# A new instruction order for an attention and mixing kernel, from a planner with other prices for changes between matmul kinds, and a fifth warm-up matmul

## The chip, the cores and the metric

The kernel runs on one core of a Trainium2 chip. The metric is device time in microseconds (us), from the first instruction to the last, for one execution. Five engines work beside each other and wait for one another by semaphores: TensorE (PE in the profile, with PEld for its weight loads), VectorE (DVE), ScalarE (ACT), GpSimd (POOL) and SyncE (SP), which here only issues transfers.

## What is computed

Four sequences of 448 tokens, twelve heads of 64, model width 768. Causal attention gives `x`, and a mixing layer follows it:

```python
scores = scale * np.matmul(q, k.transpose(0, 1, 3, 2))      # q, k, v: (4, 12, 448, 64)
scores = np.where(mask, -1000000000.0, scores)              # causal
attn = np.exp(scores - np.max(scores, axis=-1, keepdims=True))
attn = attn / (np.sum(attn, axis=-1, keepdims=True) + 1e-09)
x = np.matmul(attn, v)                                       # laid out as (4, 448, 768)

theta = x @ w_theta
zr, zi = x * np.cos(theta), x * np.sin(theta)
y = np.einsum('ts,bsd->btd', w_tok_r, zr) + np.einsum('ts,bsd->btd', w_tok_i, zi)
u = x + y
out = u + np.maximum(u @ w_ch, 0.0)
```

## The kernel before

**Attention** goes by quads, four heads at a time, three quads to a sequence, twelve in all (`load_quad`, `attend`). `load_quad` issues the transfers of a quad on SP (line 498): two tiles of q (`qs`), two of k (`kk`), two of v (`vs`), each with a pair of heads; of the first quad the q tiles come in two parts, columns 0 to 255 and 256 to 447. `attend` then makes the scores in seven blocks of 64 query rows, in four groups (`SG`): every block is four matmuls on quarters of the array, 64 by 64, two heads by two key halves (line 638, into `s`, `t` or `m` tiles of PSUM; the program calls this kind "q"). DVE adds the mask and finds the row bound (line 647, with a second small instruction that reads the accumulator), ACT takes the exponential and the row sum (line 650). PE transposes the results (line 683, kind "t", four 128 by 128 transposes into one `t` tile, of which there are two), ACT (line 515) or DVE (line 517) copies each `t` tile into `pta` or `ptb`, and PE multiplies by v (line 713, kind "x", 64 columns of the array for each of `pta` and `ptb`, into the one `xo` tile). The row sums go another way: ACT adds a small number (line 658), DVE takes the reciprocal (line 659), PE transposes it (line 660), DVE copies it to `rs` (line 661), and two transfers, `rd` and `rb`, spread it over the partitions. DVE multiplies `xo` by `rb` into `xT` (line 716) and so frees `xo` for the next pair.

**Weights** come as 64-bit floats. `weight` brings one block (`raw`), and ACT (line 539) and DVE (lines 542 twice, 545) make 32-bit floats of it (`zw`); a rounded high part is cast (line 515 or 517) and the rest is subtracted (line 523, POOL or DVE). The six blocks of `w_theta` and the seven of `w_tok` are decoded while attention runs.

**The layer**: `theta` multiplies by `w_theta` (line 766, `th`, kind "m"), then follow the sine and cosine, transposes of x (lines 825 and 826, `xp`, kind "t"), products on DVE (828, 830), a split into high and low parts (`zh`, `zl`), the token mixing (line 845, `y`, kind "m"). `pair` makes the last product (lines 943 and 953, `cp`) for two sequences together with fewer block products, and writes the output.

**The order.** Nothing of this order is written out by hand. Each operation is given to `P.op` with its engine or a choice of engines, its duration, and a due time; `Plan.order` plays the operations through once, each engine taking the ready one with the earliest due time, and the resulting list is issued as it stands. `SHIFT` moves the due time of a group of operations, `PEN` says how willingly a group is given to its second engine. `TURN` is the price in ns that the planner adds when PE goes from one kind of matmul to another (rows and columns in the order m, t, x, q), and it prefers a ready operation whose change is cheaper among those nearly as early. `QO` is an extra per score block, `gp` the price of a two-operand instruction on POOL, `tab` the activation table that ACT holds at the start, and `NW` the number of warm-up matmuls (`warm`, line 1041: 16 by 256 on zeros), which PE runs before the first scores.

Of the kernel before, what the change touches and what calls it, by code (L numbers as in the profile page):

```python
# [24 lines left out]
          PR=2, AE=19487.722, BB=6550.4261, AP=172724.4184, AQ=41305.8643, XT=3, NQ=8, WP=2, NW=4, EX=-0.0, PORT=1,  # L25
# [9 lines left out]
QO = 15.0  # L35
TURN = ((0, 0, 145, 288), (0, 0, 145, 288), (106, 56, 0, 87), (108, 120, 54, 0))


SHIFT = {2: 99415, 3: 9107, 4: -2529, 5: -6011, 6: -4744, 7: -5690, 8: 36879, 9: -6000, 10: 1863, 11: 9305, 12: 767, 13:
# [157 lines left out]
class Plan:  # L197
# [67 lines left out]
    def order(self):  # L265
# [15 lines left out]

        free = {}
        port = wire = 0.0
        tab = [None]
        last = ["m"]

        def turn(a, b):
# [37 lines left out]
        while done < len(self.ops):  # L325
# [3 lines left out]
            while ev and ev[0][0] <= t:  # L329
                _, kind, _, x = heapq.heappop(ev)  # L330
# [63 lines left out]
def attention_moe_kernel(  # L394
# [22 lines left out]
    NQ = NP // 2  # L417
# [71 lines left out]
    def gp(n):  # L489
        return 2.2 * n + 300  # L490
# [664 lines left out]
```

## Time and profile before

| | us |
|---|---|
| median of three runs | 441.61 |
| the three runs | 441.84, 441.20, 441.61 |
| the profiled execution, its own time | 441.63 |
| its span in the profile | 439.8 |
| PE busy in the span | 425.3 (97%) |
| DVE busy | 358.7 (82%) |
| ACT busy | 241.8 (55%) |
| POOL busy | 55.1 (13%) |
| mean granted TensorE clock | 0.992 |

The span counts from the first to the last instruction of the profile; 1.8 us of the execution's own time lie around it. A matmul in 32-bit floats is shown as one or two records, and a record's duration reaches from its start to the end of its passage through the array, so that records overlap: what one instruction costs PE is read from the start of one to the start of the next. The share of busy time of an engine says nothing of single stages.

### The profile page before, as it was taken

What the parts mean: (1) busy time and instruction counts of PE and PEld (TensorE: products, weight loads), DVE (VectorE), ACT (ScalarE), POOL (GpSimd) and SP (SyncE); (2) the same over time, 40 slices, a digit from 0 to 9 for tenths busy, and PEclk for the clock granted to TensorE, in tenths of its full rate; (3) what the DMA queues carried; (4) which work ended last, traced back from release to release, by engine and by line L of the source; (5) the groups of instructions that cost most, each with busy time, mean ns of one, the idle gap of its engine ahead of it and who ended that gap; (6) DMA issues with size and microseconds to landing.
All of it is one profiled execution on the core that took longest, in us unless ns stands there. A gap on an engine that the chain in (4) does not pass through costs nothing.

```text
span 439.8 us, 8190 instructions
## 1 busy us (share of the span) xinstructions
PE 425.3 (97%) x2927; PEld 354.3 (81%) x2927; DVE 358.7 (82%) x928; ACT 241.8 (55%) x602; POOL 55.1 (13%) x48
## 2 busy tenths in 40 slices
PE   8679999999999999999999999999999999999996
PEld 4347766969996686788899878979999879999995
DVE  3889999688986668679993679869569998799886
ACT  3789999389836547486830589624054533233220
POOL 2131123000000000000000000006012323231420
PEclk9889999999999999999999999999999999999999
DMA  7866785313547235152323110331533312035214
GB/s 241 306 205 232 240 255 177 106 43 109 178 148 239 87 109 165 58 163 67 99 94 143 55 57 12 110 102 36 179 110 89 104 57 90 2 105 175 98 43 146
DMA packets 33953, 55.34 MB, mean 126 GB/s; under 512 B 10361, under 2 KB 27641, under 8 KB 33913
## 3 DMA queue, kind: packets, MB, share of 16 engines
q1 hardware_dynamic: 33912, 54.82, 38.9%
q8 instruction: 23, 0.38, 0.3%
q14 instruction: 18, 0.14, 0.1%
HBM read 41.55 MB, written 11.69 MB: 121 GB/s over the span
## 4 chain that ended last, share of the span: by engine, by line
PE 86%; DVE 9%; DMA 2%; issue 1%; ACT 1%; SPq 0%; DVEq 0%; ACTq 0%
PE y L845 22%; PE th L766 20%; PE cp L943 15%; PE xo L713 10%; PE t L683 8%; PE s L638 4%; PE t L638 4%; PE xp L825 2%; DVE e L647 2%; DMA raw<-w_theta 1%; DMA qs<-q 1%; DVE R L788 1%; DVE C L828 1%; DVE zw L542 1%; DVE zl L523 1%
## 5 line engine op out<-in xcount | busy, mean ns | idle before, releaser
L766 PE MATMUL th<-wth,xs 128*128 128x384 f32 x528 | 106.1, 344 | 0.0
L845 PE MATMUL y<-wtk,zh 128*128 128x448 f32 x336 | 98.1, 373 | 0.5 <-DVE R L830 0.5
L766 PEld LDWEIGHTS th<-wth,xs 128*128 128x128 f32 x528 | 90.1, 188 | 5.2 <-issue 3.3
L650 ACT ACTIVATE e<-e,sm 128x64 f32<-128x64 f32 (+6 forms) x168 | 83.3, 498 | 17.5 <-DVE sm L647 17.3
L845 PEld LDWEIGHTS y<-wtk,zh 128*128 128x128 f32 x336 | 60.9, 188 | 5.7 <-issue 0.8
L845 PE MATMUL y<-wtk,zl 128*128 128x448 f32 x168 | 61.5, 366 | 0.0
L683 PE MATMUL t<-ident,e 128*128 128x128 f32 x336 | 48.4, 280 | 5.2 <-ACT e L650 3.2
L713 PE MATMUL xo<-pta,vs 128*64 128x448 f32 (+1 forms) x192 | 48.8, 394 | 2.3 <-DVE xT L716 2.3
L713 PE MATMUL xo<-ptb,vs 128*64 128x448 f32 (+1 forms) x192 | 48.8, 394 | 0.0
L683 PEld LDWEIGHTS t<-ident,e 128*128 128x128 f32 x336 | 39.5, 143 | 10.8 <-issue 2.4
L713 PEld LDWEIGHTS xo<-pta,vs 128*64 128x64 f32 x192 | 24.4, 139 | 27.3 <-issue 14.9
L943 PE MATMUL cp<-ub,wth 128*128 128x448 f32 x207 | 45.1, 366 | 0.0
L943 PEld LDWEIGHTS cp<-ub,wth 128*128 128x128 f32 x207 | 38.8, 188 | 3.1
L647 DVE CUSTOM_DVE_ANT_0 e<-s,mask 128x64 f32<-128x64 f32 (+3 forms) x96 | 31.2, 366 | 10.2 <-PE s L638 10.0
L943 PE MATMUL cp<-ub,wa 128*128 128x448 f32 x162 | 37.0, 366 | 0.0
L523 POOL TENSOR_TENSOR ub<-xT,ub 128x448 fp32r<-128x448 f32 x5 | 12.0, 2402 | 180.2 <-DVE ub L517 170.6
L845 PEld LDWEIGHTS y<-wtk,zl 128*128 128x128 f32 x168 | 31.5, 188 | 2.9
L943 PEld LDWEIGHTS cp<-ub,wa 128*128 128x128 f32 x162 | 30.2, 188 | 2.2
L650 ACT ACTIVATION_READ_ACCUMULATOR e<-e,sm 128x1 f32 x168 | 31.5, 188 | 0.0
L647 DVE CUSTOM_DVE_ANT_0 e<-t,mask 128x448 f32<-128x448 f32 (+2 forms) x60 | 27.3, 498 | 0.8 <-PE t L638 0.5
L515 ACT CAST ub<-tt 128x448 fp32r<-128x448 f32 x19 | 10.6, 567 | 30.2 <-PE cp L943 17.0
L638 PE MATMUL s<-kk,qs 64*64 64x64 f32 (+3 forms) x384 | 24.7, 368 | 1.1 <-DMA qs<-q 1.0
(108 smaller groups left out, 670.9 us busy)
## 6 DMA issues: line engine op xcount, KB each, us to landing
vs<-v SPq DMA_DIRECT2D x24, 256.0 KB
kk<-k SPq DMA_DIRECT2D x24, 224.0 KB
rb<-rd SPq DMA_DIRECT2D x48, 112.0 KB
qs<-q SPq DMA_DIRECT2D x22, 224.0 KB
raw<-w_theta SPq DMA_DIRECT2D x6, 768.0 KB
raw<-w_ch SPq DMA_DIRECT2D x6, 768.0 KB
wd<-zc SPq DMA_DIRECT2D x6, 768.0 KB
wf<-wd SPq DMA_DIRECT2D x24, 192.0 KB
```

Of the source, the lines that this page charges most:

```text
L515: alts.append((e, ac(n, 0 if psum else 1), lambda: nc.scalar.copy(out=o(), in_=i())))
L523: P.op([(e, gp(n) if e == "POOL" else dv(n), lambda e=e: ENG[e].tensor_tensor(out=o(), in0=a(), in1=b(), op=op)) for e in engs], r=r, w=w, ...
L542: P.op("DVE", dv2(n) + 20, lambda i=i, c=c, op=op: nc.vector.tensor_scalar(out=half(z.t[:, 1], 2)[:, :, i], in0=half(raw.t, 4)[:, :, 2 * i ...
L638: nc.tensor.matmul(out=ss[a].t[D * i:D * i + D, c:c + w], lhsT=qp[i].t[own, D * x:D * x + D], rhs=kp[i].t[own, S - w:S] if a else kp[i].t[ ...
L647: P.op("DVE", dv(w) + 8, lambda a=a, c=c, w=w, y=y, e=e, s=ss[a]: nc.vector.tensor_tensor_reduce(out=e.t[:, w * a:w * a + w], in0=s.t[:, c ...
L650: P.op("ACT", ac(w, 2.5), lambda a=a, w=w, y=y, e=e: nc.scalar.activation(out=e.t[:, w * a:w * a + w], in_=e.t[:, w * a:w * a + w], func=A ...
L683: nc.tensor.transpose(ps.t[:, 128 * y:128 * y + 128], E[x].t[:, c:c + 128], ident)
L713: nc.tensor.matmul(out=xo.t[D * a:D * a + D, 128 * j:S], lhsT=vs[i].t[:, c:c + D], rhs=pt[a].t[:, i, D * SLOT[j]:D * SLOT[j] + w], start=( ...
L766: nc.tensor.matmul(out=th.t[:, 0:HW], lhsT=l, rhs=wth[:, p, w2, c0:c0 + HW], start=(p == 0 and n == 0), stop=(p == KD - 1 and n == len(ops ...
L825: nc.tensor.transpose(xp.t[:, t], x.t[:, g, 128 * t:128 * t + 128], ident)
L845: nc.tensor.matmul(out=y.t[:, 0:S], lhsT=l.t[:, c], rhs=wtk[:, c, w2], start=(c == 0 and n == 0), stop=(c == NTK - 1 and n == 2))
L943: nc.tensor.matmul(out=banks[m].t[:, 0:S], lhsT=wt()[:, c, w2, 128 * m:128 * m + 128], rhs=ub[c].t[:, a], start=(first and c == 0 and n == 0),
```

## The change

The prices of the planner are changed, and `SHIFT` and `PEN`, more than a thousand numbers, are found anew under them. In `TURN` a change from products or transposes to scores goes from 288 to 133, from scores to products from 108 to 203, to transposes from 120 to 156, to the multiplication by v from 54 to 150; from that to scores from 87 to 40; the others by 3 at most. A score block costs 6 ns instead of 15 over its columns, and every operation of scores 9 more. `gp` falls by 125 ns. ACT is taken to hold the table of the exponential at the start. There are five warm-up matmuls instead of four. What is computed, tile shapes, buffers and the functions that issue instructions stay as they were.

```diff
-          PR=2, AE=19487.722, BB=6550.4261, AP=172724.4184, AQ=41305.8643, XT=3, NQ=8, WP=2, NW=4, EX=-0.0, PORT=1,
+          PR=2, AE=19487.722, BB=6550.4261, AP=172724.4184, AQ=41305.8643, XT=3, NQ=8, WP=2, NW=5, EX=-0.0, PORT=1,
...
-QO = 15.0
-TURN = ((0, 0, 145, 288), (0, 0, 145, 288), (106, 56, 0, 87), (108, 120, 54, 0))
+QO = 6.0
+TURN = ((0, 0, 147, 133), (3, 0, 143, 133), (106, 56, 0, 40), (203, 156, 150, 0))
...
-SHIFT = {2: 99415, 3: 9107, 4: -2529, 5: -6011, 6: -4744, 7: -5690, 8: 36879, 9: -6000, 10: 1863, 11: 9305, 12: 767, 13:
...
-PEN = {4: 14105, 6: -5988, 8: -17504, 10: -1225, 12: -4027, 14: -5212, 16: 10353, 18: -857, 20: 29527, 22: 9693, 24:
+PEN = {4: 14011, 6: -4283, 8: -21466, 10: 1214, 12: -2598, 14: -5271, 16: 10668, 18: -2831, 20: 31481, 22: 10238, 24:
...
-        tab = [None]
+        tab = ["exp"]
...
-        return 2.2 * n + 300
+        return 2.2 * n + 175
...
-            P.op("PE", c0 / 0.6 + QO * len(g), mm, rd, [(z, x) for z in ss for x in g], mode="q")
+            P.op("PE", c0 / 0.6 + 9 + QO * len(g), mm, rd, [(z, x) for z in ss for x in g], mode="q")
```

**The first transfers.** On SP, at the program's start, before the change (the numbers tell tiles apart: `qs_112` and `qs_114` are q of the first quad's two pairs, `kk_107` and `kk_109` its k, `qs_117` belongs to the second quad):

```order
L498 DMA kk_107<-k 128x448
L498 DMA kk_109<-k 128x448
L498 DMA qs_112<-q 128x256
L498 DMA qs_114<-q 128x256
L498 DMA qs_117<-q 128x448
L498 DMA qs_112<-q 128x192
L498 DMA qs_114<-q 128x192
```

And with the change (here `qs_109` and `qs_112` are q of the first quad, `kk_107` and `kk_120` its k, `qs_114` is of the second quad):

```order
L498 DMA kk_107<-k 128x448
L498 DMA qs_109<-q 128x192
L498 DMA qs_112<-q 128x256
L498 DMA qs_114<-q 128x448
L498 DMA qs_109<-q 128x256
L498 DMA qs_112<-q 128x192
L498 DMA kk_120<-k 128x448
```

The same seven transfers are issued, but the second pair's k has moved from the second place to the seventh.

**ACT between the first quad's exponentials.** Before (`zw` is a weight block being decoded, `t_238` the first quad's third group of transposes; the exponentials are named by block, `e1` to `e6`):

```order
L650 ACTIVATE e6_175,sm_149<-e6_175,sm_149 128x448 x2
L650 ACTIVATE e1_188,sm_149<-e1_188,sm_149 128x128
L539 ACTIVATE zw_209<-raw_144 128x768
L650 ACTIVATE e1_188,sm_149<-e1_188,sm_149 128x128
L650 ACTIVATE e4_194,sm_149<-e4_194,sm_149 128x320 x2
L650 ACTIVATE e5_201,sm_149<-e5_201,sm_149 128x384
L539 ACTIVATE zw_226<-raw_146 128x768
L650 ACTIVATE e5_201,sm_149<-e5_201,sm_149 128x384
L515 COPY ptb_78<-t_238 64x2x2x2x64
L658 ACTIVATE sm_149<-sm_149 128x14
```

And with the change, at the same place:

```order
L650 ACTIVATE e1_188,sm_156<-e1_188,sm_156 128x128 x2
L650 ACTIVATE e4_194,sm_156<-e4_194,sm_156 128x320 x2
L539 ACTIVATE zw_216<-raw_131 128x768
L515 COPY pta_77<-t_211 128x2x256
L650 ACTIVATE e6_179,sm_156<-e6_179,sm_156 128x448 x2
L539 ACTIVATE zw_232<-raw_133 128x768
L650 ACTIVATE e5_205,sm_156<-e5_205,sm_156 128x384
L515 COPY pta_77<-t_235 64x2x2x2x64
L650 ACTIVATE e5_205,sm_156<-e5_205,sm_156 128x384
L658 ACTIVATE sm_156<-sm_156 128x14
```

The blocks that the first transposes need stand ahead of the widest one, and ACT makes two of the copies into `pta` and `ptb` instead of one; DVE has one copy fewer there.

**PE at the third quad.** Before (`s` and `m` are score tiles, `th` a product):

```order
L638 MATMUL s<-kk,qs 64x256 x4
L638 MATMUL s<-kk,qs 64x192 x4
L638 MATMUL s<-kk,qs 64x64 x4
L638 MATMUL m<-kk,qs 64x384 x4
L638 MATMUL m<-kk,qs 64x128 x4
L766 MATMUL th<-wth,xs 128x384 x6
```

And with the change:

```order
L638 MATMUL m<-kk,qs 64x384 x4
L638 MATMUL m<-kk,qs 64x128 x4
L766 MATMUL th<-wth,xs 128x384 x6
L638 MATMUL s<-kk,qs 64x256 x4
L638 MATMUL s<-kk,qs 64x192 x4
L638 MATMUL s<-kk,qs 64x64 x4
```

Two groups of scores that stood together now have a product between them.

## Rows read from the trace of the kernel before

**Rows 1.** Page, part 1: busy us, share of the span, instructions.

```profile
PE 425.3 (97%) x2927; PEld 354.3 (81%) x2927; DVE 358.7 (82%) x928; ACT 241.8 (55%) x602; POOL 55.1 (13%) x48
```

**Rows 2.** Busy by stretch: length, then PE, PEld, DVE, ACT, POOL, clock, DMA share, GB/s.

```profile
0.00:34.00 34.00, 25.41 (x190) 14.94 (x190) 22.73 (x87) 21.95 (x69) 8.52 (x14) 0.90 0.75 253
34.00:434.60 400.60, 398.78 (x2733) 338.62 (x2732) 334.22 (x837) 219.82 (x534) 46.60 (x34) 1.00 0.36 115
...
16.50:19.90 3.40, 3.31 (x32) 2.23 (x36) 2.31 (x6) 1.38 (x4) 1.11 (x1) 0.50 0.42 169
30.20:33.50 3.30, 3.30 (x20) 2.38 (x17) 1.46 (x7) 0.88 (x4) 1.52 (x1) 0.50 1.01 351
```

**Rows 3.** PE in order of time, first 36 us: start, duration, instruction, idle before.

```profile
0.78 3.57 PE L1041 MATMUL warm<-const-float32-0.0 128*16 128x256 f32 x8 [0.78 <-PEq L1146]
5.32 2.21 PE L638 MATMUL s<-kk,qs 64*64 64x256 f32 x18 [0.96 <-DMA qs<-q]
...
17.64 1.99 PE L638 MATMUL s<-kk,qs 64*64 64x256 f32 x24
19.40 1.30 PE L638 MATMUL m<-kk,qs 64*64 64x384 f32 x16
...
29.42 0.59 PE L713 MATMUL xo<-pta,vs 128*64 128x448 f32 x1 [2.25 <-DVE xT L716]
...
34.72 1.10 PE L638 MATMUL s<-kk,qs 64*64 64x256 f32 x24
35.64 1.05 PE L638 MATMUL m<-kk,qs 64*64 64x384 f32 x16
```

**Rows 4.** SP in order of time, the first seven transfers.

```profile
0.75 0.87 SPq L498 DMA_DIRECT2D kk<-k  x2
1.67 2.32 SPq L498 DMA_DIRECT2D qs<-q  x5
```

**Rows 5.** DVE in order of time, 7 to 33 us.

```profile
7.85 0.22 DVE L647 CUSTOM_DVE_ANT_0 e<-s,mask 128x64 f32<-128x64 f32 x1 [6.82 <-PE s L638]
...
15.86 0.68 DVE L517 COPY pta<-t 128x512 f32<-128x512 f32 x1
16.46 0.68 DVE L517 COPY ptb<-t 128x512 f32<-128x512 f32 x1
17.75 0.68 DVE L517 COPY pta<-t 64x512 f32<-64x512 f32 x1 [0.61 <-PE t L683]
...
19.31 0.24 DVE L659 RECIPROCAL sm<-sm 128x14 f32<-128x14 f32 x1 [0.38 <-ACT sm L658]
...
28.76 0.61 DVE L716 TENSOR_TENSOR xT<-xo,rb 128x448 f32<-128x448 f32 x1
```

**Rows 6.** ACT in order of time, the copy after the first quad's exponentials.

```profile
18.46 0.58 ACT L515 COPY ptb<-t 64x512 f32<-64x512 f32 x1 [1.38 <-DVE pta L517]
```

**Rows 7.** PE in order of time, 37 to 44 us.

```profile
37.79 1.04 PE L683 MATMUL t<-ident,e 128*128 128x128 f32 x8
38.76 0.77 PE L638 MATMUL s<-kk,qs 64*64 64x320 f32 x8
39.46 0.79 PE L766 MATMUL th<-wth,xs 128*128 128x384 f32 x3
40.09 1.03 PE L683 MATMUL t<-ident,e 128*128 128x128 f32 x8
40.88 1.81 PE L766 MATMUL th<-wth,xs 128*128 128x384 f32 x9
42.62 0.98 PE L638 MATMUL t<-kk,qs 64*64 64x448 f32 x8
43.53 0.59 PE L713 MATMUL xo<-pta,vs 128*64 128x448 f32 x1
```

**Rows 8.** PE's waits after 34 us (total, times, longest); PE's last row.

```profile
PE xp L825 <- DVE R L830: 0.5, 2, 0.4
435.59 0.59 PE L953 MATMUL cp<-ub,wth 128*128 128x224 f32 x3 [0.48 <-DVE u L977]
```

More of the change, by code (lines that the diff above doesn't have):

```diff
@@ L34 @@
 ROOM = (("s", "t", "s", "t"), ("s", "m", "s", "t"))
-QO = 15.0
-TURN = ((0, 0, 145, 288), (0, 0, 145, 288), (106, 56, 0, 87), (108, 120, 54, 0))
-SHIFT = {2: 99415, 3: 9107, 4: -2529, 5: -6011, 6: -4744, 7: -5690, 8: 36879, 9: -6000, 10: 1863, 11: 9305, 12: 767, 13:
[113 rows of a table removed]
-PEN = {4: 14105, 6: -5988, 8: -17504, 10: -1225, 12: -4027, 14: -5212, 16: 10353, 18: -857, 20: 29527, 22: 9693, 24:
[27 rows of a table removed]
+QO = 6.0
+TURN = ((0, 0, 147, 133), (3, 0, 143, 133), (106, 56, 0, 40), (203, 156, 150, 0))
+SHIFT = {2: 71693, 3: 5616, 4: -7916, 5: -16183, 6: -6173, 7: -10324, 8: 14353, 9: -12559, 10: 1178, 11: 9449, 12: 1108,
[113 rows of a table added]
+PEN = {4: 14011, 6: -4283, 8: -21466, 10: 1214, 12: -2598, 14: -5271, 16: 10668, 18: -2831, 20: 31481, 22: 10238, 24:
[27 rows of a table added]
 class Buf:
```

280 rows, old and new, of tables (PEN, SHIFT) are left out of this document.

## The prediction

> **What bounds the kernel now.** I read the page's busy times first: PE is busy for 97% of the span, DVE for 82% [rows 1]. Such a PE leaves little idle time, so I asked where it lies. The table by stretches says that 8.6 us of it fall in the first 34 us (25.4 busy of 34), and 1.8 us in the next 400.6 [rows 2]. The first stretch is worse than its idle time shows, because the clock is low in parts of it: 0.50, which is 1.2 GHz, from 16.5 to 19.9 us and from 30.2 to 33.5 us, with PE busy all through both [rows 2]. It was also low at the start, by the pace of the work: 18 of the first group's 24 score records take 2.21 us there, as slow as 24 in 1.99 us later at 1.2 GHz [rows 3]. A score group of 256, 192 and 64 columns takes 1.76 us at 1.2 GHz (17.64 to 19.40) and 0.92 at 2.4 (34.72 to 35.64), and the first quad's scores, 1792 columns, takes 6.2 us at the first pace and 3.2 at the second [rows 3].
>
> Then I went through PE, SP, DVE and ACT in order of time. PE waits for the first transfers until 5.32 us, and for DVE's product from 27.2 to 29.42 us, 2.25 us [rows 3]. DVE gets its first scores at 7.85 us and is then the engine that the others wait for; its own waits up to that product at 28.76 are 0.61 and 0.38 us and a few tenths [rows 5]. ACT waits 1.38 us once, before its copy at 18.46 [rows 6]. So three places can give or take time: the start, up to 34 us, set by the first transfer and by the row of work on DVE; the 400 us after it, set by PE's own work with short waits in it; and the end, where the last product waits 0.48 us for DVE and DVE then finishes alone [rows 8].
>
> **Part 1, PE's changes between kinds.** Counted in the two programs, PE changes its kind 204 times before and 185 times after. The price is in the trace. Eight transposes take 0.79 us where a product follows (40.09 to 40.88) and 0.97 where scores follow (37.79 to 38.76): going into scores costs 0.18 more than into a product. A block of 448 columns takes 0.91 us up to the next kind (42.62 to 43.53), one of 320 columns 0.70 (38.76 to 39.46); the 128 columns between them cost 0.21, so the columns alone are 0.74 and 0.53, and 0.17 is left for going out of scores, whatever comes next [rows 7]. A visit to the scores thus costs 0.35 us in all; the old table charged 288 + 108 = 396 ns with a product on both sides, the new one 133 + 203 = 336. The 22 changes that fall away for good are those between products and transposes (121 before, 99 after). Eight transposes between two products cost 0.79 us, which is about 0.1 a piece with nothing added, so these 22 give back 0. The changes that cost something, into and out of scores and the product with v, go from 83 to 86; at the 0.17 of the scores that would be 0.5 us lost, and if the six more that end in transposes are as cheap as going from transposes to a product, nothing. I take +0.1, nearer to the lower end, because those six are the ones that grew; bounds 0 and +0.5.
>
> **Part 2, the start.** The first group of scores needs q and k of both pairs. Before, these are the first four transfers; after, the second pair's k is the seventh. SP issues one each 0.46 us (0.75 to 1.67 for two), the fourth at 2.13 and the seventh at 3.55 [rows 4]. The third, issued at 1.67, was used at 5.32 [rows 3, 4], that is 3.65 us later; the seventh then serves at 7.2, and scores and DVE's first instruction come 3 x 0.47 = 1.4 us later than before: 9.3 us instead of 7.85 [rows 5]. What pays for this is the order behind it. DVE makes three copies of transposed tiles instead of four up to its first product (0.60 us each by their starts, 15.86 to 16.46 [rows 5]), because ACT takes one more, and ACT has 1.38 us of waiting to take it from [rows 6]. The two waits of DVE, 0.61 for transposes and 0.38 for the row sums, should go, since the blocks that the first transposes need now stand ahead of the widest one on ACT, and DVE comes to them later. So DVE arrives at the product of 28.76 with +1.4 - 0.6 - 0.6 - 0.4 = -0.2 us. Bounds: if no wait is saved, +0.8; if the few tenths beside the two go as well, -0.5. Otherwise DVE has the same instructions up to there, 71 against 72, and the row sums, whose transfers go behind it on SP, keep their places. The product frees `xo`, for which PE sits idle, so its 0.2 us is PE's 0.2; and PE then works at 1.2 GHz from 30.2 us on [rows 2], so that what it does earlier it does at 2.4, in half the time. I take -0.3 for the start.
>
> The fifth warm-up matmul costs 3.57 / 4 = 0.89 us of PE and ends at 5.24, ahead of the scores even as they stood before (5.32) [rows 3]. It is hidden by the transfer; with scores as early as their second transfer allowed, it would cost up to 0.89.
>
> **Part 3, the waits behind it.** From 34 us to 434.6 us PE is idle for 1.8 us in rows, the largest of them for DVE's products and copies (`xp`, 0.5) [rows 2, 8]. Others may be hidden in overlapping records, where these rows don't show them. What changes here is DVE's load: of the copies of transposed tiles DVE makes 41 before and 35 after, ACT 55 and 61, and two subtractions of `w_theta` blocks go to POOL. Six copies at 0.6 are 3.6 us that DVE no longer has in front of PE's needs, while ACT is busy for 55% [rows 1]. I take 0.8 us for the waits that go, less than half of the 1.8; bounds -1.8 (all of them go) and +1.5 (as many new ones come as there are now). The end is as it was: the last six trios of matmuls and the DVE instructions after them stand in the same order, and the 0.48 us stays [rows 8].
>
> **The sum** is made against the profiled execution's 441.63, which is 0.02 from the median of the three runs (441.61): +0.1 - 0.3 - 0.8 = -1.0, **440.6 us**.
>
> **The rivals.** First, that nothing is gained: the waits move and don't shrink, and what falls away are the changes that cost nothing. For it speaks that PE's own work is the same to 0.1 us and that DVE and PE are both nearly full up to 60 us. It gives 441.6, with a range of 441.2 to 442.1.
>
> Second, a slower one, by the late transfer. Before, PE had worked from 5.32 us on when its clock rose; now it has nothing from 5.24 to 7.2. If the rise comes later for that, the first quad's scores run wholly at 1.2 GHz, 6.2 us from 7.2 to 13.4 [rows 3], instead of ending near 11.4. DVE, which by its own row would be at the fifth block at 11.9, waits for it about 1.4 us, and so does everything that hangs on DVE up to 29.4: -0.3 becomes +1.1 to +1.4, and the time 442.2 to 443.2, say 442.7. It decides itself by whether the rise comes ahead of the last third of these scores.
>
> Third, a faster one, by the same clock the other way round: the fall at 30.2 us follows PE's idle stretch of 2.25 us [rows 2, 3], and if that is a little shorter the fall may not come, or the longer warm-up brings the first rise forward. 3.3 us of full work at half the clock [rows 2] hold 1.65 us of gain: 439.0. The Trainium skill (TensorE: Matmul & The Clock Gate, Part 1) says that the activity monitor runs freely and isn't reset when a kernel starts, so that the place of a rise differs between executions of one kernel. By that rule the second and third rival could both come up in different runs; the three runs before, within 0.64 us, don't show such a spread.
>
> Fourth, new waits in the middle: the transposes that take a `t` tile again while its copy is still going stand as close as before, and as copies queue on ACT behind exponentials instead of on DVE, two or three may come late by 0.5 each: 442.5 to 443.2.
>
> **How the numbers follow.** Forecast 0.35 (439.9 to 441.1), nothing gained 0.25, clock gained 0.16, late clock 0.16, new waits 0.08. A measurement of this kernel can tell about 0.2%, 0.9 us, from no change. Faster by more than that, below 440.7: six tenths of the forecast, all of the clock's gain and a little of the second case, 0.41. Within 0.9 us: 0.35. Above 442.5: most of the late clock and of the new waits, 0.24. The range leaves out the tip of the clock's gain below 438.9 and the worst of the slower cases above 443.1.
>
> **What would show it.** PE's first scores start at about 7.2 us, DVE's first instruction at 9.3, and DVE's first `xT` product at 28.6; if that one is past 29.5, part 2 is wrong. The clock rises before 11 us. Eight transposes with scores behind them still take 0.97 us. In the stretch from 34 us to the last product PE's idle time is near 1 us instead of 1.8; if it is 2 or more, part 3 is wrong, and the first rival or the fourth holds.

## The result: 1.3% slower, against a forecast of 0.2% faster

| | before | after |
|---|---|---|
| median | 441.58 us (441.20 to 441.84, 4 runs) | 446.62 us (445.74 to 449.42, 4 runs) |
| ratio, 95% interval | | 1.0126 [1.0081, 1.0171] |
| profiled execution, its span | 441.63, 439.8 | 449.42, 447.6 |

The profiled execution of after is the longest of its four; a second one, taken later (e9 below), has 446.92 us, the shortest of its six, and a span of 445.1. Both are read here, so that an accident of one isn't taken for the change.

PE is busy a little longer and is 96% instead of 97% full, as the page's first part says (compare [rows 1]):

```profile
PE 429.8 (96%) x2929; PEld 354.3 (79%) x2929; DVE 357.9 (80%) x928; ACT 244.8 (55%) x605; POOL 48.2 (11%) x45
```

The busy times by stretch (columns as in [rows 2]) say where PE stands still. Up to 34 us it is busy for 25.46 us, as before (25.41). The clocks of that row, 0.80 and 0.90 in [rows 2], can't be compared: a stretch without a record counts as 1.00, and the trace has none ahead of the clock's first rise, at 3.44 us here and at 9.7 us before, though the pace of the work is low until then. From 34 to 442.4 us it is idle for 408.40 - 403.22 = 5.2 us, where [rows 2] had 1.8 in nearly the same length; 2.0 of them lie between 120 and 170 us, 0.7 between 34 and 70.

```profile
0.00:34.00 34.00, 25.46 (x184) 14.09 (x185) 20.64 (x82) 22.01 (x69) 8.24 (x14) 0.80 0.70 226
34.00:442.40 408.40, 403.22 (x2740) 339.45 (x2740) 335.54 (x843) 222.82 (x536) 40.00 (x32) 1.00 0.37 115
34.00:70.00 36.00, 35.27 (x306) 24.10 (x306) 33.04 (x117) 31.79 (x92) 9.43 (x7) 1.00 0.77 245
120.00:170.00 50.00, 47.98 (x370) 38.77 (x368) 34.92 (x103) 24.41 (x73) 1.01 (x1) 1.00 0.44 143
```

The start, in PE's, SP's and DVE's rows in order of time (columns as in [rows 3 to 5]): the second pair's k, issued at 3.55 us, lets PE go on at 8.01, DVE's first instruction comes at 10.11, its first product with the row sums at 31.31, and PE's product with v after it at 31.97, where before had 5.32, 7.85, 28.76 and 29.42.

```profile
0.78 3.62 PE L1041 MATMUL warm<-const-float32-0.0 128*16 128x256 f32 x10 [0.78 <-PEq L1146]
6.25 0.61 PE L638 MATMUL s<-kk,qs 64*64 64x256 f32 x2 [1.84 <-DMA qs<-q]
8.01 1.45 PE L638 MATMUL s<-kk,qs 64*64 64x256 f32 x13 [1.15 <-DMA kk<-k]
...
14.16 0.52 PE L683 MATMUL t<-ident,e 128*128 128x128 f32 x3
...
31.97 0.59 PE L713 MATMUL xo<-pta,vs 128*64 128x448 f32 x1 [2.25 <-DVE xT L716]
```
```profile
0.74 0.39 SPq L498 DMA_DIRECT2D kk<-k  x1
1.19 2.32 SPq L498 DMA_DIRECT2D qs<-q  x5
3.55 0.43 SPq L498 DMA_DIRECT2D kk<-k  x1
```
```profile
10.11 0.23 DVE L647 CUSTOM_DVE_ANT_0 e<-s,mask 128x64 f32<-128x64 f32 x1 [9.07 <-PE s L638]
...
31.31 0.61 DVE L716 TENSOR_TENSOR xT<-xo,rb 128x448 f32<-128x448 f32 x1
```

Among PE's waits (engine, line waited for, total us, times, longest) there is one of 1.6 us, where before had 0.5 at most for that line, and waits of transposes for copies on ACT (the one of 0.8 is at 17.10, in the start). The end is as it was [rows 8]: the last product waits 0.48 us, at 443.41.

```profile
PE y L845 <- DVE R L830: 1.6, 1, 1.6
PE t L683 <- ACT ptb L515: 1.2, 3, 0.5
PE t L683 <- ACT pta L515: 0.8, 1, 0.8
```

### The profile page after: what moved, and what is told of

It is laid out like the page before. It is cut to its first block, busy times and chain, and to the rows that moved or that the text cites. A ratio compares the mean times of both kernels' runs of the same rounds, so it can differ in the third digit from the quotient of the medians.

```text
span 447.6 us, 8177 instructions
## 1 busy us (share of the span) xinstructions
PE 429.8 (96%) x2929; PEld 354.3 (79%) x2929; DVE 357.9 (80%) x928; ACT 244.8 (55%) x605; POOL 48.2 (11%) x45
## 4 chain that ended last, share of the span: by engine, by line
PE 75%; DVE 11%; DMA 6%; ACT 3%; issue 2%; SPq 1%; POOL 1%; DVEq 0%
PE th L766 19%; PE y L845 16%; PE cp L943 14%; PE xo L713 8%; PE t L683 6%; PE s L638 4%; PE t L638 4%; DVE zl L523 2%; DMA raw<-w_ch 2%; DMA rd<-rs 1%; DMA wf<-wd 1%; PE xp L825 1%; SPq L498 1%; DVE e L647 1%; DVE tt L523 1%
## 5 line engine op out<-in xcount | busy, mean ns | idle before, releaser
L766 PE MATMUL th<-wth,xs 128*128 128x384 f32 x528 | 103.6, 343 | 0.5 <-DVE xs L749 0.5
L713 PE MATMUL xo<-pta,vs 128*64 128x448 f32 (+1 forms) x192 | 47.5, 387 | 2.3 <-DVE xT L716 2.2
L713 PE MATMUL xo<-ptb,vs 128*64 128x448 f32 (+1 forms) x192 | 47.5, 387 | 0.0
L943 PE MATMUL cp<-ub,wth 128*128 128x448 f32 x207 | 46.0, 369 | 0.0
L638 PE MATMUL s<-kk,qs 64*64 64x256 f32 (+3 forms) x384 | 25.8, 372 | 3.3 <-DMA qs<-q 1.8
L523 POOL TENSOR_TENSOR ub<-xT,ub 128x448 fp32r<-128x448 f32 x5 | 7.7, 1559 | 186.1 <-DMA raw<-w_ch 164.7
L515 ACT CAST ub<-tt 128x448 fp32r<-128x448 f32 x17 | 9.5, 568 | 28.9 <-PE cp L943 15.7
```

What stands on the lines that cost most here:

```text
L515: alts.append((e, ac(n, 0 if psum else 1), lambda: nc.scalar.copy(out=o(), in_=i())))
L523: P.op([(e, gp(n) if e == "POOL" else dv(n), lambda e=e: ENG[e].tensor_tensor(out=o(), in0=a(), in1=b(), op=op)) for e in engs], r=r, w=w, ...
L638: nc.tensor.matmul(out=ss[a].t[D * i:D * i + D, c:c + w], lhsT=qp[i].t[own, D * x:D * x + D], rhs=kp[i].t[own, S - w:S] if a else kp[i].t[ ...
L713: nc.tensor.matmul(out=xo.t[D * a:D * a + D, 128 * j:S], lhsT=vs[i].t[:, c:c + D], rhs=pt[a].t[:, i, D * SLOT[j]:D * SLOT[j] + w], start=( ...
L766: nc.tensor.matmul(out=th.t[:, 0:HW], lhsT=l, rhs=wth[:, p, w2, c0:c0 + HW], start=(p == 0 and n == 0), stop=(p == KD - 1 and n == len(ops ...
L943: nc.tensor.matmul(out=banks[m].t[:, 0:S], lhsT=wt()[:, c, w2, 128 * m:128 * m + 128], rhs=ub[c].t[:, a], start=(first and c == 0 and n == 0),
```

## The experiments

Both plans consist of the same steps with the same dependences; they differ in order, and in the engine of 164 of the 2177. So for the experiments the plan is written out as a list of steps with their engines, which takes the place of the planner's run (`order = replay(P)` for `order = P.order()`), and single entries of the list are moved. All of them ran beside the kernel before, in three groups: e1 to e4 and e5 to e8 on one chip, e9 to e12 on another. Its medians there are 442.75, 442.76 and 442.31 us, about 1 us above that of the first comparison. So the ratios are to be compared, and absolute times in the expectations stand some 1 us low. After itself ran in the third group alone, so that what e1 to e7 gain against it (e9) is a difference across two chips. "PE idle" is PE's idle time between 34 and 420 us in the kernel's one profile (before: 1.8, the first profile of after: 5.2).

| kernel | median us | ratio to before, 95% interval | PE idle, us |
|---|---|---|---|
| e9, after itself | 448.54 | 1.0137 [1.0109, 1.0164] | 3.7 |
| e1, start of before, rest of after | 446.29 | 1.0069 [1.0042, 1.0096] | 5.5 |
| e2, start of after, rest of before | 442.68 | 1.0002 [0.9978, 1.0027] | 2.4 |
| e3, after with four warm-ups | 446.76 | 1.0098 [1.0059, 1.0137] | 4.5 |
| e4, after with before's first transfers | 446.06 | 1.0082 [1.0050, 1.0113] | 4.9 |
| e5, after, decoding later | 446.85 | 1.0106 [1.0071, 1.0141] | 4.6 |
| e6, after, four groups of transposes later | 446.14 | 1.0092 [1.0067, 1.0117] | 3.1 |
| e7, e5 and e6 together | 444.99 | 1.0058 [1.0030, 1.0085] | 1.8 |
| e10, e7 with e4 and two more moves | 441.90 | 0.9989 [0.9973, 1.0004] | 1.2 |
| e8, start of e4, rest of before | 441.16 | 0.9977 [0.9952, 1.0002] | 1.7 |
| e12, e8 with four warm-ups | 440.95 | 0.9970 [0.9947, 0.9993] | 1.9 |
| e11, e8, four groups of PE later | 440.56 | 0.9963 [0.9946, 0.9979] | 1.1 |

### Start or rest: e1 and e2

After the first 140 steps (about 33 us) both plans have done the same 140, so they can be joined there.

```diff
 e1
+ORDER = before[:140] + [step for step in after if step not in before[:140]]    # NW=4
 e2
+ORDER = after[:140] + [step for step in before if step not in after[:140]]     # NW=5
```

> The first 140 steps of the plan (up to about 33 us: loads, first two quads) in the order of the kernel before, with its four warm-up matmuls; the rest in the order of after. Both orders have done the same 140 steps there, so nothing is cut through. Theory 'start' (the 4 to 5 us are lost up to 34 us, by the late transfer of the second pair's k and the clock): 441 to 442.5 us, and the profile's PE work behind 35 us runs as in before. Theory 'rest' (new waits and slower matmuls behind 34 us): 445 to 447 us.

> The reverse: the first 140 steps and five warm-up matmuls of after, the rest in the order of before. Theory 'start': 445 to 447 us. Theory 'rest': 440.5 to 442.5 us.

The order behind the start is the larger loss: with before's start it still costs 3.1 us (1.0069), and after's start with before's rest costs nothing that can be measured (1.0002). The theory "start" as the whole cause falls. The two ratios add up to half of e9's 0.0137 only. That a start costs more ahead of the one rest than of the other isn't shown by it: e9 ran on the other chip, and against the first comparison (1.0126) the difference lies within the three intervals.

The profiles can be parted at the third quad's first scores, where PE has done the same work in either order and 2734 of its records are still to come.

| | PE at the third quad, us | from there to the end, us |
|---|---|---|
| before | 34.72 | 405.1 |
| e1 (start of before) | 34.97 | 410.6 |
| e2 (rest of before) | 35.54 | 406.7 |
| after, e9 | 35.77, 35.20 | 411.8, 409.9 |

```profile
35.77 1.09 PE L638 MATMUL m<-kk,qs 64*64 64x384 f32 x16
```
```profile
35.20 1.09 PE L638 MATMUL m<-kk,qs 64*64 64x384 f32 x16
```

By these single executions after's start comes 0.2 to 1.1 us later than before's, and after's rest takes some 5 us longer (3 to 7).

### Inside the start: e3 and e4

```diff
 e3
-KN = dict(... NW=5 ...)
+KN = dict(... NW=4 ...)          # the order stays
 e4, SP's first rows
-L498 DMA kk<-k 128x448
-L498 DMA qs<-q 128x192
-L498 DMA qs<-q 128x256
+L498 DMA kk<-k 128x448 x2
+L498 DMA qs<-q 128x256 x2
 L498 DMA qs<-q 128x448
-L498 DMA qs<-q 128x256
-L498 DMA qs<-q 128x192
-L498 DMA kk<-k 128x448
+L498 DMA qs<-q 128x192 x2
```

> The order of after word for word, with four warm-up matmuls instead of five. Theory 'warm-up' (the fifth brings the clock up early, at 3.4 us, so that it falls again at 6.85 while PE waits for transfers): the clock is granted at full before the transposes at 14 us and the time is 443 to 445. Theory 'hidden' (the warm-up matmul lies beside transfers and does nothing): 445.5 to 447 us.

> The order of after, but SP's first seven transfers stand as in before: the second pair's k second instead of seventh, the next quad's q fifth. Theory 'late transfer': first scores done some 1.5 to 2.5 us earlier, DVE's first product with the row sums (after: ends about 31.9) earlier by 1 to 2 us, time 443 to 445 us. Theory 'rest': the start gains that and the time falls by no more than 1 us, 445 to 446.5.

e3: without the fifth warm-up matmul the time is still 1.0098, with an interval that reaches after's 1.0137, and its profile has a clock of 0.55 from 6.85 to 13.68 us, not the full one that the theory "warm-up" expects. By the time alone a share in the loss isn't excluded; e8 and e12 below bear on that. e4: against e9 the order of the first seven transfers is worth 0.0055, or 2.4 us, as the theory "late transfer" expects, at the edge of what the two intervals part; against e3, on the same chip, it is 0.7 us, and e8 against e2, which differ in it ahead of before's rest, 1.1 us. The profile of e4 shows the mechanism in PE's and DVE's rows: the first scores at 5.21 us without a wait, 24 records in 1.54 us, DVE's first instruction at 6.89 and its product at 27.90. PE comes to the third quad at 33.63 us.

```profile
5.21 1.54 PE L638 MATMUL s<-kk,qs 64*64 64x256 f32 x24
```
```profile
6.89 0.23 DVE L647 CUSTOM_DVE_ANT_0 e<-s,mask 128x64 f32<-128x64 f32 x1 [5.86 <-PE s L638]
27.90 0.61 DVE L716 TENSOR_TENSOR xT<-xo,rb 128x448 f32<-128x448 f32 x1
```

### In the middle: e5, e6, e7

To find the places, I took PE's starts in each profile and compared the distance of each two with the same pair's usual distance. Four profiles of after's rest (after, e1, e3, e4) show waits at the same places of the work: near 87, 157, 201 and 262 us before transposes (0.48, 0.58, 0.72 and 0.66 us over the usual distance, equal to 0.02 in all four), near 307 and 371 before products (0.7 to 0.8 and 0.5), and one near 126 us that is 1.8, 1.9 and 1.3 us long and in e3 not there.

The one at 126 us, in after's rows of SP, DVE and PE in order of time:

```profile
115.39 1.14 SPq L498 DMA_DIRECT2D rb<-rd  x2
116.63 0.53 SPq L498 DMA_DIRECT2D raw<-w_ch  x1
117.22 1.08 SPq L498 DMA_DIRECT2D rb<-rd  x2
118.40 0.53 SPq L498 DMA_DIRECT2D sp<-xT  x1
```
```profile
121.19 0.60 DVE L851 TENSOR_TENSOR xT<-y,xT 128x448 f32<-128x448 f32 x1
123.56 1.11 DVE L542 TENSOR_SCALAR zc<-raw 128x768 uint16<-128x768 uint16 x2 [1.76 <-DMA raw<-w_ch]
...
126.95 0.68 DVE L828 TENSOR_TENSOR C<-xp,C 128x512 f32<-128x512 f32 x1
127.55 0.54 DVE L830 TENSOR_TENSOR R<-xp,R 128x384 f32<-128x384 f32 x1
```
```profile
128.24 0.44 PE L845 MATMUL y<-wtk,zh 128*128 128x448 f32 x1 [1.60 <-DVE R L830]
```

DVE stands for 1.76 us in front of the decoding of a w_ch tile, because that tile's transfer, issued between those of the row sums, takes from 116.63 to 123.5, 6.9 us. L828 and L830, whose products free the tile that PE waits for, are queued behind it. The length depends on the transfer: in e9 it lands 5.5 us after its issue, DVE waits 0.33 us there and PE's start is 0.34 late.

The one at 157 us, in PE's, DVE's and ACT's rows:

```profile
155.85 1.03 PE L683 MATMUL t<-ident,e 128*128 128x128 f32 x8
...
157.83 1.26 PE L683 MATMUL t<-ident,e 128*128 128x128 f32 x8 [0.42 <-ACT ptb L515]
```
```profile
156.49 0.68 DVE L517 COPY pta<-t 64x512 f32<-64x512 f32 x1
```
```profile
157.20 0.58 ACT L515 COPY ptb<-t 64x512 f32<-64x512 f32 x1 [1.18 <-DVE pta L517]
```

The mixed tile of transposes (its partitions 0 to 63 go to `pta`, 64 to 127 to `ptb`) is copied in two halves, which the planner takes for independent. In the trace the second starts when the first has ended (156.49 + 0.68 = 157.17), since the built program gives it that wait, both reading one PSUM tile. The tile is free after some 1.3 us instead of 0.6, and the plan lets PE come back to it after only three product matmuls. The same wait stands in ACT's totals as 7.0 us in 6 places in after, 2.8 in 3 before: the new plan gives the halves to DVE and ACT, in this order, six times instead of three. To ACT and DVE, in the other order, it gives them three times instead of five, and there too the second half starts when the first has ended. So such a tile is copied one half behind the other in both kernels, and what differs is how soon PE comes back. The waits near 87 and 262 us are of the same kind; near 201 PE waits for a whole tile, whose copy stands on DVE behind an addition (L851) and starts at 200.56 us. The Trainium skill (PSUM — Partial Sum Buffer, PSUM bank collisions raise a hardware error) says that two engines may be in one bank at a time if they touch different 32-partition quadrants, and that guarding by whole banks is the simple version. The two halves touch different quadrants. No run here took that wait away.

```diff
 e5, DVE's rows near 122 us (ACT's L539 and the next tile's pieces are moved likewise)
-L542 TENSOR_SCALAR zc<-raw 128x768 x2
 L517 CAST zh<-R 128x384
-L545 SCALAR_TENSOR_TENSOR zc<-zc 128x768
 L523 TENSOR_TENSOR zl<-C,zh 128x512
 L523 TENSOR_TENSOR zl<-R,zh 128x384
 L828 TENSOR_TENSOR C<-xp,C 128x4x128
 L830 TENSOR_TENSOR R<-xp,R 128x3x128
+L542 TENSOR_SCALAR zc<-raw 128x768 x2
+L545 SCALAR_TENSOR_TENSOR zc<-zc 128x768
 e6, PE's rows near 157 us (at 87, 201 and 262 us likewise)
 L766 MATMUL th<-wth,xs 128x384 x3
+L766 MATMUL th<-wth,xs 128x384 x3
 L683 MATMUL t<-ident,e_1712 128x128    (8 rows of transposes)
-L766 MATMUL th<-wth,xs 128x384 x3
```

> After's order with one thing moved: the decoding of the two first w_ch tiles (ACT L539, DVE L542 and L545; and the issue of the second tile's transfer, which needs the first's buffer) stands behind the product L830 (for the second: L851) that PE needs, instead of ahead of it. Theory 'a DVE queue that stands behind a transfer': DVE no longer sits 1.8 us behind the 768 KB transfer near 122 us with the products behind it, PE's wait of 1.4 to 1.9 us near 125 us goes, and the time falls by 1.3 to 1.8 us against after, to 444 to 445.3. Theory 'slow matmuls' (the loss is the pace of PE's own matmuls, 206.7 instead of 202.7 ns a 448-column one): within 0.5 us of after.

> After's order, only PE's row changed at four places: the group of transposes that waits for its tile's copy near 87, 157, 201 and 262 us stands behind the next trio (at one place two) of product matmuls. Theory 'tiles taken too soon' (the two half copies of the mixed tile run one behind the other, which the plan doesn't know): these four waits of 0.5 to 0.7 us go, 2.4 us in all, and the time falls by 1.5 to 2.4 us. Theory 'slow matmuls': within 0.5 us of after. If the copies then become late for the products with v, less than 1 us is gained.

> Both edits together. If the two kinds of waits are what the new order loses, the gains add up: 3 to 4 us below after, 442.3 to 443.7, near the kernel before. If the waits only move, the sum is clearly less than the two single gains.

By the times, e5 gains 0.0031 against after (1.4 us) and e6 0.0045 (2.0), either no more than the two intervals allow by chance; together in e7 it is 0.0079, 3.5 us, which the intervals of e7 and e9 do separate, though across the two chips. In the profiles each wait goes where it should. In e5, DVE's decoding comes at 125.50 without a wait behind L830, and PE has no wait there:

```profile
125.04 0.55 DVE L830 TENSOR_TENSOR R<-xp,R 128x384 f32<-128x384 f32 x1
125.50 1.09 DVE L542 TENSOR_SCALAR zc<-raw 128x768 uint16<-128x768 uint16 x2
```

In e6 the wait of 0.42 us becomes one of 0.17 for a later copy; near 201 and 262 us none is left.

```profile
157.45 0.66 PE L683 MATMUL t<-ident,e 128*128 128x128 f32 x4 [0.17 <-DVE ptb L517]
```

That the gains add fits waits that end on PE and don't just move on. Against "slow matmuls" as the cause speak the profiled executions of e10 and e11 below: they have the slower pace at the end (206.7 ns) and spans of 441.2 and 438.3 us, e9 has the faster one and 445.1.

### The whole sum: e9 and e10

```diff
 e10: e7, e4's transfers, and near 307 us on DVE (a second exchange, of two product blocks near 371 us, is on PE)
-L542 TENSOR_SCALAR zc<-raw 128x768 x2
 L851 TENSOR_TENSOR xT<-y,xT 128x448 x2
+L542 TENSOR_SCALAR zc<-raw 128x768 x2
```

> The changed kernel itself, unchanged, beside the others on this chip, as the measure of what the repairs give. Its ratio to before should be 1.009 to 1.013. Its second profile tells which waits belong to the order: theory 'order' expects again the waits near 87, 157, 201, 261 and 307 us within 0.1 us of the first profile's, and the one behind the w_ch transfer near 125 us at 1 to 2 us; theory 'accident of one execution' expects them elsewhere.

> After's order with before's first seven transfers, both earlier repairs (decoding behind the products, four groups of transposes later), and two more: the second w_ch decoding near 307 us behind the additions L851 that free the tile PE waits for, and near 371 us one product block exchanged with its neighbour. Theory 'waits of the order and the late transfer are the whole loss': within 0.2% of before, 442 to 443.5 on this chip. If 1.5 us or more are still missing against before, something else is lost that these repairs don't touch.

e9's ratio, 1.0137, is just over what was expected. It has the waits near 87, 157, 201 and 262 us within 0.01 us of the first profile's and the one near 307 within 0.2; the one near 126 us, expected at 1 to 2 us, was 0.34. So the former are the order's, the latter hangs on the transfer. e10 is after's plan with the transfers of e4 (2.4 us by its ratio), the two kinds of waits of e7 (3.5) and two smaller ones mended, and it takes 0.9989 of before's time: the loss of 0.0137 is gone, within the interval. PE's idle time between 34 and 420 us falls from 3.7 to 1.2 us with it.

That the waits and the late transfer are the whole loss doesn't follow, for e10's start is better than before's. PE comes to the third quad at 33.28 us, 1.4 earlier than in before, and takes 407.9 us from there, of which it is busy for 402.6. In e11 below, on the same chip, with before's rest and the same slower pace at the end, these are 406.0 and 400.8. So some 1.9 us of the rest's loss are left in these two profiles (1 us in the medians of e10 and e12), in what the rows show as PE's busy time and not in waits that they show. The first scores of the third quad and the rest from there, as in [rows 3] and [rows 2], in e10 and in e11:

```profile
33.28 1.09 PE L638 MATMUL m<-kk,qs 64*64 64x384 f32 x16
33.28:441.20 407.92, 402.62 (x2734) 339.24 (x2733) 335.48 (x840) 221.29 (x534) 39.94 (x31) 1.00 0.37 115
```
```profile
32.26 1.10 PE L638 MATMUL s<-kk,qs 64*64 64x256 f32 x24
32.26:438.30 406.04, 400.76 (x2734) 339.04 (x2733) 335.47 (x839) 218.74 (x532) 46.73 (x34) 1.00 0.37 116
```

### A version that beats both: e8, e12, e11

```diff
 e8
+ORDER = after[:140] with e4's transfers + [the other steps as in before]    # NW=5
 e12: e8 with NW=4
 e11: e8, PE's rows near 144 us (near 179, 194 and 344 us likewise)
 L766 MATMUL th<-wth,xs 128x384 x3
+L766 MATMUL th<-wth,xs 128x384 x3
 L683 MATMUL t<-ident,e_1732 128x128    (8 rows of transposes)
-L766 MATMUL th<-wth,xs 128x384 x3
```

> The first 140 steps of after with before's order of the first seven transfers and five warm-up matmuls, then before's order. In the profile of after with these transfers PE reached the same work at 35 us 1.2 us earlier than before did, and the order of before behind it keeps the later waits short. Theory 'the start is worth something': 440 to 440.8 us, faster than before by 0.8 to 1.5. Theory 'the start only wins time that later waits eat, or it was the clock of that one execution': 441.3 to 442.

> The best order so far with four warm-up matmuls instead of five, nothing else. If the fifth is hidden beside transfers: within 0.2% of the same order with five (0.9977 of before). If it is what keeps PE's clock up in the first scores: 1 to 2 us more, 1.000 to 1.002.

> The best order so far (start of after with before's transfers, five warm-up matmuls, before's order behind it) and, on PE's row alone, three groups of transposes and one xp group that wait in before (near 144, 179, 194 and 344 us, 0.48, 0.48, 0.30 and 0.32 us) moved behind the next product. Theory 'tiles taken too soon' holds for before's order too: 1 to 1.5 us below the same kernel without the moves, 0.993 to 0.996 of before. If such waits only move on: no difference to it.

e8's interval reaches 1.0002, so alone it isn't shown to be faster; e11 is, at 0.9963 [0.9946, 0.9979], 1.6 us below before and 8.0 below after (e9) on the same chip. Five and four warm-ups give the same (0.9977 and 0.9970), and the first scores start at 5.43 and 5.40 us, so the fifth is hidden. e11 against e8 gains 0.6 us, less than the 1 to 1.5 expected and, across the two chips, not separable by time; PE's idle time falls by 0.6 us too, to 1.1.

## Why the prediction was wrong

**Part 1, the changes between kinds (+0.1): the prices held, the sum was too small.** In after, eight transposes with a product behind them take 0.79 us (41.59 to 42.38) and a block of 448 columns 0.91 up to the next kind (44.69 to 45.60), both as in [rows 7]. Going from a product into scores has a price too, which the sum lacked: three products take 0.70 us ahead of scores (42.38 to 43.08) and 0.63 ahead of transposes (39.46 to 40.09 [rows 7]). Behind 35 us after does it 13 times, before 5 times. And all scores together, from each start to the next, take 35.2 us there in after and e9, 34.3 to 34.6 in before, e2, e11 and e12. With the changes that fall away this comes to about +0.6, an estimate from these starts, just over the bound of +0.5.

```profile
41.59 1.04 PE L683 MATMUL t<-ident,e 128*128 128x128 f32 x8
42.38 0.77 PE L766 MATMUL th<-wth,xs 128*128 128x384 f32 x3
43.08 0.77 PE L638 MATMUL s<-kk,qs 64*64 64x320 f32 x8
...
44.69 0.98 PE L638 MATMUL t<-kk,qs 64*64 64x448 f32 x8
45.60 0.48 PE L713 MATMUL xo<-pta,vs 128*64 128x320 f32 x1
```

**Part 2, the start (-0.3): wrong.** It came out at +0.2 to +1.1 us by PE's start at the third quad. The gain by the order behind the transfer was there: with before's transfers the new start is at the third quad 1.1 us earlier than before in e4 and 1.9 in e8 (32.87). The price of the late transfer was not 1.4 but some 2 (after 35.77 and e9 35.20 against 33.63 in e4; e2 35.54 against e8). Two steps failed. The seventh transfer was given the 3.65 us from issue to use that the third needed; it took 8.01 - 3.55 = 4.46, with six others issued ahead of it. And the scores were taken to get the full clock before 11 us. In the first profile they didn't: the clock was granted at full from 3.44 us, while the last warm-ups ran, then 0.50 from 6.85 to 13.68 us, after PE had stood idle for the transfers, and the scores took 6.15 us, 8.01 to 14.16. That is the second rival, with its 6.2 us.

```profile
3.44:6.85 3.41, 1.56 (x7) 0.39 (x5) 0.00 (x0) 0.00 (x0) 0.23 (x1) 1.00 0.86 241
6.85:13.68 6.83, 5.68 (x55) 3.91 (x54) 2.66 (x18) 2.79 (x13) 0.00 (x0) 0.50 0.97 376
```

In e9, the same kernel, that stretch has 0.75:

```profile
6.85:13.68 6.83, 4.75 (x55) 3.23 (x56) 3.55 (x23) 3.29 (x16) 0.00 (x0) 0.75 0.97 345
```

Seven profiles have this start (after, e9, e2, e5, e6, e7, and e3 with four warm-ups). In e9 and e7 the clock is at full again by 10.7 us and the product comes at 29.47 and 29.17. In the other five the scores run almost wholly at the low pace and it comes at 30.97 to 31.96; three of these (e2, e5, e6) have no rise during the warm-ups at all, the first at 13.2 to 13.5 us. By the rule of the Trainium skill (TensorE: Matmul & The Clock Gate, Part 1) cited for the third rival, that the monitor runs freely, executions of one kernel should differ in this way, and these do. What should pay for the late transfer, fewer copies and waits on DVE, gives 9.3 to 28.6, 19.3 us, in the prediction; e9 has that (10.13 to 29.47), the first profile 21.2 (10.11 to 31.31). The mark set for part 2, the product past 29.5, was passed in five of the seven. The fifth warm-up was hidden, as said.

**Part 3, the waits behind it (-0.8): wrong in sign, and the largest error.** The idle time was to fall from 1.8 to 1 us and rose to 5.2 and 3.7; from the third quad to the end after takes 411.8 and 409.9 us where before takes 405.1. The step that failed is the one from DVE's load to PE's waits: six copies fewer on DVE were counted as relief for PE. What decides is which instruction stands last ahead of PE's need. The plan took the halves of the mixed tile for independent and came back to it too soon at three places, and at a fourth too soon for a copy of a whole tile on DVE (about 2 us, e6). Before has waits of the first kind as well (0.48, 0.48 and 0.30 us near 144, 179 and 194, which e11 moves), so only half of these 2 us is a difference between the kernels. And the plan set an instruction that waits for a transfer ahead of instructions that PE waits for (0 to 1.9 us near 126), and one that doesn't near 307 (0.7 to 0.9).

**The rivals.** The fourth, new waits in the middle, named the transposes that take a tile again while it is being copied; it was given 0.08 and two or three places at 0.5 us. It came with three of these and one of another kind, behind the other half's copy and not behind exponentials, and with DVE's queue behind a transfer, which I had not looked for. And the second and the fourth were priced as alternatives, each against 441.6. Both came, and the range had no case for their sum. That sum, about 444 from their own prices, would still have been some 2.6 us short.

**Open.** What the 1 to 2 us are that e10 leaves in the rest; the scores take 35.9 us from start to start in e10 and 34.6 in e11, which is 1.3 of them. And which input of the planner (the prices of the changes, the score's length, POOL's price or the two tables) made the order worse: they were changed together, and no run parts them.

## What to carry to other kernels

When a new order is weighed, go through the row of each engine that PE waits for and ask of every instruction that can wait for a transfer who is queued behind it: it belongs behind what the bound engine needs. A planner that leaves out a wait the program has (here two halves of one tile, copied one behind the other) can use that slack up; put such a wait into it before its prices are refined (that a planner with it does better was not tried). And rivals that don't exclude each other have to be added, not only set side by side.

## What was not expected of the hardware

**Two paces of the same matmuls.** In after the 36 last full-width matmuls take 7.60 us, in e9, the same program, 7.46:

```profile
433.65 7.60 PE L943 MATMUL cp<-ub,wth 128*128 128x448 f32 x36
```
```profile
431.31 7.46 PE L943 MATMUL cp<-ub,wth 128*128 128x448 f32 x36
```

With the last one's own 0.37 us taken off, that is 206.6 and 202.7 ns apiece, at a granted clock of 1.00 in both. Such a pace holds through uninterrupted work: in after from about 393 us to the end, in before 202.7 from about 360. Over 50 us that is 1 us, and it differs between executions of one program. Both paces come on one chip (e10, beside e9, has 7.60 us for these 36) and in one execution (e2: 206.7 ns from 360 to 400 us, 202.7 from 420). What sets it was not tried.

**Spread.** e11's ten runs lie within 0.71 us (440.03 to 440.74), e8's twelve within 5.6 (438.94 to 444.51), at mean granted clocks of 0.986 to 0.992 and 0.986 to 0.995. Only four groups of PE's row differ, and the chip. The chip alone isn't it: e12, e8's order with four warm-ups on e11's chip, spreads over 5.3 us. That isn't explained.
